# First expert slot prepared during stage one, slot table shared with GpSimd, half slots split like full ones

## The chip, the cores and the metric

The kernel runs on one core of one Trainium2 chip. The metric is the device time of one execution in microseconds; for the kernel before, the median of three runs.

## The reference

Two parts follow each other. The first is a linear-attention recurrence over 768 steps for 4 batches and 8 heads of 40 columns; its output, read as 3072 tokens of 320 columns, is the input x of the second, a mixture of 8 experts with one expert per token:

```
logits = x @ w_gate + modality_bias[modality_id]
e_idx  = argmax(logits, axis=1)
probs  = softmax(logits)          # 1e-09 added to the denominator
gate_w = probs[arange(N), e_idx]
for e in range(8):                # tokens whose expert is e
    h = maximum(x[mask] @ w1[e], 0.0)        # w1[e]: 320 x 1024
    out[mask] = gate_w[mask, None] * (h @ w2[e])   # w2[e]: 1024 x 320
```

All is float32.

## The kernel before, in words

**Stage one** (`phase_a`) computes the recurrence in 24 chunks. Its operations are not issued as they are written: each call is recorded with its operands, and a list scheduler (`Sched.order`) plans all five engines with assumed costs, by the length of the work that follows each operation, and then issues them in that order. Tiles come from rings; a ring made by `late` hands out tiles of stage one that are done with. After every pair of chunks, `gate` (line 990) computes the expert of 256 tokens and scatters their rows, from GpSimd, into a table `xs` in DRAM that is sorted by expert.

**The expert stage** (`_run`, line 1128) works in slots. A full slot is 256 tokens of one expert, a half slot 128. The slots are numbered from -2: slots -2 and -1 are chosen early, at pair 8 of stage one (`early`, line 1076), from the experts that already have 256 tokens; slot 0 after pair 10; slots 1 to 9 (full), 10 and 11 (half) come from a slot table. Slots past 11 stand under a condition at the end (line 1237 on).

A full slot is computed with float32 split in two rounded parts (float32r, high and low), three products for one. `split` (line 1157) makes the parts: for each 128 tokens three transposes of x on TensorE (line 1169) into PSUM, ScalarE copies the high part xh (1171), VectorE subtracts for the low part xl (1172, 1173). For the weights ScalarE copies h (1176, 1180, 1184) and VectorE subtracts for l (1177, 1181, 1185), in pieces named a, b (w1) and c (w2), or q (quarters of w1, for the first slot of a group). Two c pieces of slot -2 are subtracted on GpSimd. The pieces of the next slot are put between the f-steps of the present one by the lists `plan0`, `plan1` and `plan`.

One f-step is 128 of the 1024 hidden columns: `g1` is eight products of 256 columns (line 1201), ScalarE's relu hh (1205), VectorE's low part hl (1206); `g2` is six products of 320 columns (1213 to 1215). `g2` runs two f-steps behind `g1`. `fin` (1216) scales the sum and scatters the rows to the output from GpSimd.

Half slots (`h1`, `h2`, lines 1190 to 1195) are not split: plain float32 products, three of 128 columns and one of 320 for each f-step; TensorE runs a plain float32 product in two instructions.

The slot table (`slots`, line 1031) is 44 small operations on VectorE from the counts of tokens by expert (`cnt`, line 1230). They are issued between the f-steps of slot -2, 15 at a time (`tb`). SP reads the table (`tabi`) for the addresses of slot 1 on.

Slot -2's weights and x are loaded during stage one into the tiles XT0 and BK0 to BK3 (hence their names in the profile), but split only after stage one. Slot -1's weights are loaded when stage one has ended.

Of the kernel before, what the change touches and what calls it, by code (L numbers as in the profile page):

```python
# [71 lines left out]
class Sched:  # L72
# [408 lines left out]
def phase_a(S,ctx,rt,rm,bk,v,w,a,emit_x,pp,ident,kp):  # L481
# [16 lines left out]
    def tiles(name,n,shape,cp=cp): return [cp.tile(shape,F32,name=f"{name}{i}") for i in range(n)]  # L498
# [416 lines left out]
NTL=NT//128; SL=256; NSF=12; NSL=NSF+E; NX0=3; NF0=9; NHF=2  # L915
# [8 lines left out]
class Moe:  # L924
# [106 lines left out]
    def slots(self,ct):  # L1031

        nc=self.nc; V=nc.vector; T=lambda nm,shape,dt=F32: self.wp.tile([128]+shape,dt,name="s_"+nm,bufs=1); NB=NT//SL
# [6 lines left out]
        def run(i):  # L1040
# [3 lines left out]
        le=[lambda k=k,sl=sl,n=n: V.tensor_tensor(c2[:,sl],cur[3][:,k:k+1].broadcast_to([128,n,E]),self.f2[:,0:n].unsqueeze(2).broadcast_to([128,n,E]),op=ALU.is_le) for k,sl,n in part]  # L1044
        return [lambda: V.memset(n0[:,E:],0.0),lambda: V.memset(nh[:,E:],0.0),
            lambda: V.tensor_copy(n0[:,0:E],ct),
            lambda: V.tensor_tensor(n1,ct,self.used[:,0:E],op=ALU.subtract),
            lambda: V.tensor_scalar(m1,n1,-SL/2.0,None,op0=ALU.add),
            lambda: V.tensor_tensor(c1,m1.unsqueeze(2).broadcast_to([128,E,NB]),self.f1.unsqueeze(1).broadcast_to([128,E,NB]),op=ALU.is_gt),
            lambda: V.tensor_reduce(nb[:,0],c1,axis=AX.X,op=ALU.add),  # L1050
            lambda: V.scalar_tensor_tensor(m1,nb[:,0],-float(SL),n1,op0=ALU.mult,op1=ALU.add),
            lambda: V.tensor_scalar(nb[:,1],m1,0.0,None,op0=ALU.is_gt)]+run(0)+run(1)+run(2)+[
            lambda: V.scalar_tensor_tensor(nh[:,0:E],nb[:,0],-float(SL),n0[:,0:E],op0=ALU.mult,op1=ALU.add),
            lambda: V.tensor_tensor(dn[:,0],n0[:,1:E+1],n0[:,0:E],op=ALU.subtract),
            lambda: V.tensor_tensor(dn[:,1],nh[:,1:E+1],nh[:,0:E],op=ALU.subtract),
            lambda: V.scalar_tensor_tensor(dn[:,0],nb[:,0],float(SL),dn[:,0],op0=ALU.mult,op1=ALU.add)]+le+[
            lambda: V.tensor_reduce(es,c2,axis=AX.X,op=ALU.add)]+mul+[
            lambda: V.tensor_scalar(tab[:,NSL:2*NSL],es,float(E-1),None,op0=ALU.min),
            lambda: V.tensor_reduce(s0,c2,axis=AX.X,op=ALU.add),
            lambda: V.tensor_tensor(du,self.used[:,1:E+1],self.used[:,0:E],op=ALU.subtract),  # L1060
            lambda: V.scalar_tensor_tensor(s0[:,0:NSF],self.f2,-float(SL),s0[:,0:NSF],op0=ALU.mult,op1=ALU.add),
            lambda: V.tensor_scalar(tab[:,2*NSL:],cur[3][:,1,E-1:E],float(NF0-NHF),None,op0=ALU.add),
            lambda: V.tensor_tensor(tab[:,2*NSL:],tab[:,2*NSL:],cur[3][:,0,E-1:E],op=ALU.max),
            lambda: V.tensor_scalar(s0[:,0:NSF],s0[:,0:NSF],n0[:,0:1],0.0,op0=ALU.add,op1=ALU.max),
            lambda: V.tensor_scalar(s0[:,NSF:],s0[:,NSF:],nh[:,0:1],None,op0=ALU.add),
            lambda: V.tensor_scalar(s0[:,NSF:NSF+NHF],s0[:,NSF:NSF+NHF],SL/2.0,None,op0=ALU.add)]+le+[
            lambda: V.scalar_tensor_tensor(tab[:,0:NSL],es,float(PT),s0,op0=ALU.mult,op1=ALU.add),
            lambda: V.tensor_tensor(c2,c2,du.unsqueeze(1).broadcast_to([128,NSL,E]),op=ALU.mult),
            lambda: V.tensor_copy(self.tab,tab),
            lambda: V.tensor_reduce(end,c2,axis=AX.X,op=ALU.add),  # L1070
            lambda: V.tensor_tensor(pos,bc(tab[:,0:NSL]),self.row.unsqueeze(1).broadcast_to([128,NSL,2]),op=ALU.add),
            lambda: V.tensor_scalar(end,end,self.used[:,0:1],float(SL),op0=ALU.add,op1=ALU.add),
            lambda: V.scalar_tensor_tensor(end,es,float(PT),end,op0=ALU.mult,op1=ALU.add),
            lambda: V.tensor_tensor(self.pad,bc(end),pos,op=ALU.is_gt),
            lambda: V.tensor_scalar(self.pad,self.pad,float(BIG),None,op0=ALU.mult)]
    def early(self,R):
# [17 lines left out]
        self.first[0]=(idx,xg,r1,r3,r2)  # L1094
# [31 lines left out]
    def _run(self,ctx,wpool,pool,ph,po):  # L1126
# [3 lines left out]
        W_={}; xg=[None]*4; self.wp=wpool  # L1130
        def wt(nm,i,shape,dt=F32): W_[nm,i]=(pool if i==0 else wpool).tile(shape,dt,name=f"{nm}_{i}",bufs=1)
        for i in range(2):
            xg[i]=pool.tile([128,2,XW],F32,name=f"xg{i}",bufs=1)
            wt("r1",i,[128,2,F]); wt("r3",i,[128,F]); wt("r2",i,[128,8,D])
            wt("xf",i,[128,3,128])
            for nm,sh in (("xh",[128,3,SL]),("xl",[128,3,SL]),("h1",[128,2,F]),("l1",[128,2,F]),("w3",[128,F]),("h2",[128,8,D]),("l2",[128,8,D])): wt(nm,i,sh,F32R)
            xg[2+i]=pool.tile([128,2,XW],F32,name=f"xg{2+i}",bufs=1)
        for i in range(2): nc.gpsimd.memset(W_["xl",i][64:128,2].bitcast(F32),0.0)
        def prep(s):
# [3 lines left out]
            hf=half(s); n=SL//2 if hf else SL; k=s-1 if s<=NF0 else s-1-NF0+NSF if hf else s-1-NHF if s<=NSF+NHF else s-1-NF0+NSF-(NSF-NF0)  # L1143
# [5 lines left out]
        half=lambda s: NF0<s<=NF0+NHF  # L1149
# [7 lines left out]
        def split(s,P):  # L1157
            _,x,r1,r3,r2=P
            if half(s):
                xf=W_["xf",s%2]  # L1160
                def xq():
                    tp=ph.tile([128,512],F32,tag="h",name=f"xt{s+2}")[:,0:384].rearrange("p (c t) -> p c t",c=3)
                    for c in range(3): nc.tensor.transpose(tp[0:64 if c==2 else 128,c],x[0][:,(4,132,260)[c]:(132,260,324)[c]],self.ident)
                    nc.scalar.copy(xf[:,0:2],tp[:,0:2]); nc.scalar.copy(xf[0:64,2],tp[0:64,2])
                return (xf,r1,r3,r2),dict(x=[xq],a=[],b=[],c=[],q=[])
# [42 lines left out]
        def g2(s,W,f,hx,os,bs=(0,1)):  # L1208
            if half(s): return h2(s,W,f,hx,os)
            h2_,l2=W[5:]; hh,hl=hx  # L1210
            for b in bs:
# [13 lines left out]
        def group(lo,hi):  # L1225
            P={}; W={}
            if lo<0:
# [5 lines left out]
                for f in u['x']+u['q'][:1]: f()  # L1233
# [159 lines left out]
```

## Time and profile before

| | us |
|---|---|
| runs | 701.68, 703.48, 704.94 |
| median | 703.48 |
| profiled execution | 702.02 |
| its span, first to last instruction | 700.3 |

The page lists for each engine its busy time: PE is TensorE's products, PEld its weight loads, DVE is VectorE, ACT ScalarE, POOL GpSimd, SP the engine that issues DMAs. In names, digits are left out: h and l are the high and low parts of weights, r the raw ones, BK and XT raw ones of slot -2. L391 is the line that issues everything of stage one. Ends of products are modelled; differences of starts are exact.

### The profile page before, as it was taken

To read this page: it belongs to the slowest core of one execution; us is meant where nothing else is said; L and a number is where in the kernel's file an instruction comes from. 1 tells how busy PE (TensorE), PEld (TensorE's weight loads), DVE (VectorE), ACT (ScalarE), POOL (GpSimd) and SP (SyncE) were. 2 spreads that over 40 slices of the span, in tenths; PEclk is the share of its full clock that TensorE was granted. 3 is DMA by queue.
4 is the path that set the end of the run, shared out by engine and by line. 5 is a ranking of instruction groups with operands and counts; after the bars stand their busy time and mean duration, and the time that the engine had idled before them with its cause. 6 is when DMAs were issued, how large, how long until landed. Compare 5 with 4: busy or idle time off the path is not lost.

```text
span 700.3 us, 24925 instructions
## 1 busy us (share of the span) xinstructions
PE 576.2 (82%) x10426; PEld 513.2 (73%) x10426; DVE 461.2 (66%) x1162; ACT 370.2 (53%) x802; POOL 251.5 (36%) x427
## 2 busy tenths in 40 slices
PE   0584679896987699759988987868999999999994
PEld 0473559685766588648876875747999999999972
DVE  5999954266773876395637464359988888888210
ACT  0575233375646746655567375426766666666210
POOL 9467707106958840894180201121111111211110
PEclk9986556787998869867979598757999999999998
DMA  1779422346443636432521336167686777777200
GB/s 46 292 189 239 126 56 70 75 122 184 144 133 79 201 92 148 121 108 61 120 91 44 111 74 218 59 213 204 212 285 206 229 247 230 227 240 223 97 18 12
DMA packets 95721, 102.42 MB, mean 146 GB/s; under 512 B 57775, under 2 KB 78560, under 8 KB 95456
## 3 DMA queue, kind: packets, MB, share of 16 engines
q1 hardware_dynamic: 93200, 92.82, 45.6%
q0 software_dynamic: 2400, 7.92, 3.1%
q8 instruction: 84, 1.38, 0.8%
q14 instruction: 37, 0.30, 0.1%
HBM read 86.38 MB, written 17.52 MB: 148 GB/s over the span
## 4 chain that ended last, share of the span: by engine, by line
PE 51%; DVE 12%; issue 9%; DMA 8%; ACT 4%; POOL 2%; SPq 1%; POOLq 0%; DVEq 0%; ACTq 0%
PE ps_tr L391 24%; PE h L1201 10%; PE ps_rp L391 6%; DMA out_dram<-o,oi 5%; PE os L1215 3%; PE os L1213 3%; PE os L1214 3%; DVE Z L391 2%; PE tz L391 2%; ACT XZ L391 2%; DVE BK L391 1%; PE xt L1169 1%; DMA xs<-xo,pi 1%; SPq L391 1%; DVE qx L391 1%
## 5 line engine op out<-in xcount | busy, mean ns | idle before, releaser
L391 POOL TENSOR_TENSOR tmpP<-L 128x234 f32<-128x234 f32 (+14 forms) x148 | 77.4, 526 | 127.4 <-DMA L<-scr 93.9
L1224 POOL DMA_INDIRECT out_dram<-o,oi x26 | 28.9, 1110 | 172.2 <-DVE oi L1223 97.5
L391 ACT COPY XZ<-BK 32x640 f32<-32x640 f32 x96 | 69.0, 723 | 28.2 <-PE ps_tr L391 25.1
L391 POOL TENSOR_TENSOR L<-L,tmpP 128x234 f32<-128x234 f32 (+14 forms) x148 | 79.7, 542 | 9.0
L1205 ACT ACTIVATE hh<-h 128x256 fp32r<-128x256 f32 x96 | 36.9, 385 | 64.6 <-PE h L1201 64.4
L391 DVE COPY U<-ps_tr 32x320 f32<-32x320 f32 x56 | 27.6, 492 | 52.2 <-PE ps_tr L391 44.2
L1215 PE MATMUL os<-h,hl 128*128 128x320 f32 x192 | 60.1, 313 | 0.7 <-DVE hl L1206 0.7
L1201 PE MATMUL h<-xh,h 128*128 128x256 f32 x192 | 57.3, 298 | 3.8 <-DVE hl L1206 1.5
L1213 PE MATMUL os<-h,hh 128*128 128x320 f32 x192 | 60.3, 314 | 0.0
L1214 PE MATMUL os<-l,hh 128*128 128x320 f32 x192 | 59.9, 312 | 0.0
L391 POOL DMA_INDIRECT xs<-xo,pi x24 | 23.9, 994 | 93.4 <-issue 27.4
L1206 DVE SCALAR_TENSOR_TENSOR hl<-h,hh 128x256 fp32r<-128x256 f32 x96 | 40.6, 423 | 24.2 <-ACT hh L1205 23.2
L1201 PE MATMUL h<-xh,l 128*128 128x256 f32 x192 | 55.4, 289 | 0.3 <-DVE l L1177 0.3
L1201 PE MATMUL h<-xl,h 128*128 128x256 f32 x192 | 55.2, 287 | 0.0
L391 DVE TENSOR_TENSOR MB<-ps_tr,msk 64x512 f32<-64x512 f32 x48 | 33.0, 688 | 30.5 <-PE ps_tr L391 29.8
L391 PE MATMUL ps_tr<-ident,BK 128*104 128x128 f32 x192 | 37.5, 341 | 15.3 <-DVE BK L391 9.3
L391 PE MATMUL ps_tr<-rs,TT 64*64 64x40 f32 x896 | 40.6, 253 | 4.8 <-DMA TT<-scrT 3.3
L391 ACT COPY XZ<-ps_tr 40x320 f32<-40x320 f32 x92 | 38.3, 420 | 11.7 <-PE ps_tr L391 10.4
L391 PEld LDWEIGHTS ps_tr<-rs,TT 64*64 64x64 f32 x896 | 36.5, 162 | 9.4 <-ACT rs L391 2.4
L391 ACT COPY U<-ps_tr 32x320 f32<-32x320 f32 x56 | 23.3, 416 | 37.7 <-DVE U L391 21.2
L391 ACT COPY UT<-ps_tr 104x512 f32<-104x512 f32 x48 | 26.7, 589 | 30.6 <-PE ps_tr L391 30.0
L391 PEld LDWEIGHTS ps_tr<-ident,BK 128*104 128x104 f32 x192 | 27.5, 162 | 19.4 <-DVE BK L391 8.8
(221 smaller groups left out, 1589.1 us busy)
## 6 DMA issues: line engine op xcount, KB each, us to landing
r<-in_moe_w_dram SPq DMA_DIRECT2D x13, 1280.0 KB
r<-in_moe_w_dram SPq DMA_DIRECT2D x13, 1024.0 KB
BK<-in_bk_dram SPq DMA_DIRECT2D x12, 832.0 KB
r<-in_moe_w_dram SPq DMA_DIRECT2D x26, 256.0 KB
A<-in_a_dram SPq DMA_DIRECT2D x12, 416.0 KB
U<-in_v_dram SPq DMA_DIRECT2D x48, 104.0 KB
ws<-in_w_dram SPq DMA_DIRECT2D x24, 165.5 KB
RT<-in_rt_dram SPq DMA_DIRECT2D x48, 80.0 KB
```

Of the source, the lines that this page charges most:

```text
L391: else: r=getattr(getattr(nc,eng),name)(*[rs(x) for x in a],**{n:rs(x) for n,x in k.items()})
L1169: for c in range(3): nc.tensor.transpose(tp[:,c],x[b][:,(4,132,196)[c]:(132,260,324)[c]],self.ident)
L1201: for i,(a,b) in enumerate(k): nc.tensor.matmul(hp,a,b,start=(i==0),stop=(i==len(k)-1))
L1205: nc.scalar.activation(hh,hp,AF.Relu)
L1206: nc.vector.scalar_tensor_tensor(hl,hp,0.0,hh.bitcast(F32),op0=ALU.max,op1=ALU.subtract)
L1213: nc.tensor.matmul(os[b],hh[:,sl],h2_[:,f],start=(f==0),stop=False)
L1214: nc.tensor.matmul(os[b],hh[:,sl],l2[:,f],start=False,stop=False)
L1215: nc.tensor.matmul(os[b],hl[:,sl],h2_[:,f],start=False,stop=(f==7))
L1224: nc.gpsimd.indirect_dma_start(self.out,bass.IndirectOffsetOnAxis(ap=oi.bitcast(U32),axis=0),o,None,bounds_check=NT-1,oob_is_err=False)
```

## The change

1. `early` splits slot -2's x and first-layer weights within stage one, as recorded operations. The parts go into tiles that stage one has done with: AT0 to AT3 (h1, l1 of both halves of w1), XT1 (the last 64 rows), A0 and A1 (xh, xl). These tiles move to the pool `kp`, which lives on, and are taken anew with the type float32r (`Ring.anew`). `_run` starts slot -2 with these tiles; only w2 is still split there.
2. In `slots`, 23 of the 44 operations go to GpSimd (`V`), one to ScalarE; 20 stay on VectorE (`D`). They are issued 7 instead of 15 for each f-step.
3. `h1`, `h2` and the tiles `xf` are gone: half slots are split and computed like full ones, with 128 instead of 256 columns in `g1`, `hh` and `hl`, and one block in `g2`, `fin` and the x part of `split`.
4. The loop in `group` is written more simply; a way of ending a group with a full slot, which does not occur in the group of slots -2 to 11, is left out.

```
 class Ring:
-    alias=None; prior=None
+    alias=None; prior=None; anew=None
+    def get(self,i):
+        if self.anew is not None: self.bufs=[self.anew()]; self.anew=None
+        return self.bufs[i]
...
     def early_tiles():
-        l=[('XT',0)]+[Br[i] for i in OPT['EB']]
-        return [S.late(f"e_{i}",[t]) for i,t in enumerate(l)]
+        l=[('XT',0)]+[Br[i] for i in OPT['EB']]+ATr[:4]+[('XT',1)]+Ar
+        r=[S.late(f"e_{i}",[t]) for i,t in enumerate(l)]
+        for i in range(5,12):
+            tag=f"AT{i-5}" if i<9 else "XT1" if i<10 else f"A{i-10}"; n=2*HQ if i>9 else F
+            r[i].anew=lambda i=i,tag=tag,n=n: kp.tile([128,n],F32R,name=f"er{i}",tag=tag,bufs=1)
+        return r
...
     def slots(self,ct):
-        nc=self.nc; V=nc.vector; ...
+        nc=self.nc; V=nc.gpsimd; D=nc.vector; ...
-            lambda: V.tensor_copy(n0[:,0:E],ct),
-            lambda: V.tensor_tensor(n1,ct,self.used[:,0:E],op=ALU.subtract),
+            lambda: nc.scalar.copy(n0[:,0:E],ct),
+            lambda: V.tensor_tensor(n1,n0[:,0:E],self.used[:,0:E],op=ALU.subtract),
             lambda: V.tensor_scalar(m1,n1,-SL/2.0,None,op0=ALU.add),
-            lambda: V.tensor_tensor(c1,m1.unsqueeze(2)...
-            lambda: V.tensor_reduce(nb[:,0],c1,axis=AX.X,op=ALU.add),
+            lambda: D.tensor_tensor(c1,m1.unsqueeze(2)...
+            lambda: D.tensor_reduce(nb[:,0],c1,axis=AX.X,op=ALU.add),
...
     def early(self,R):
-        self.first[0]=(idx,xg,r1,r3,r2)
+        h1=[S.inst(R[5+2*c],...)...]; l1=[...]; w3=S.inst(R[9],"w3_e",[128,F]); xh,xl=[...]
+        nc.gpsimd.memset(xl[64:128,2].bitcast(F32),0.0); fr=lambda v: v.bitcast(F32R)
+        for b in range(2):
+            tp=S.inst(S.rings['ps_tr'],f"et{b}",[128,3,128]); sl=slice(128*b,128*b+128)
+            for c in range(3): nc.tensor.transpose(tp[:,c],xg[b][:,(4,132,196)[c]:(132,260,324)[c]],self.ident)
+            nc.scalar.copy(fr(xh[:,:,sl]),tp); nc.scalar.copy(fr(xh[0:64,2,sl]),tp[64:128,2])
+            nc.vector.tensor_tensor(fr(xl[:,0:2,sl]),tp[:,0:2],xh[:,0:2,sl].bitcast(F32),op=ALU.subtract)
+            nc.vector.tensor_tensor(fr(xl[0:64,2,sl]),tp[64:128,2],xh[64:128,2,sl].bitcast(F32),op=ALU.subtract)
+        for q in range(2):
+            sl=slice(512*q,512*q+512)
+            for c in range(2):
+                nc.scalar.copy(fr(h1[c][:,sl]),r1[c][:,sl]); nc.vector.tensor_tensor(fr(l1[c][:,sl]),r1[c][:,sl],h1[c][:,sl].bitcast(F32),op=ALU.subtract)
+            nc.scalar.copy(fr(w3[:,sl]),r3[:,sl]); nc.vector.tensor_tensor(fr(w3[64:128,sl]),r3[64:128,sl],w3[64:128,sl].bitcast(F32),op=ALU.subtract)
+        self.first[0]=(idx,xg,r1,r3,r2,(xh,xl,h1,l1,w3))
...
     split:
-            if half(s): ...
-                return (xf,r1,r3,r2),dict(x=[xq],a=[],b=[],c=[],q=[])
+            if s==-2: X=A=B=Q=[]
...
-        def h1(s,W,f): ...
-        def h2(s,W,f,hh,os): ...
-        def g1(s,W,f,to=None):
+        def g1(s,W,f):
-            hp=ph.tile([128,512],F32,tag="h",name=f"h{s+2}_{f}")[:,0:SL]
+            fs=slice(128*f,128*f+128); n=size_(s); ts=slice(0,n)
+            hp=ph.tile([128,512],F32,tag="h",name=f"h{s+2}_{f}")[:,ts]
...
     group:
-                        if lo<0:
-                            for _ in range(MOPT['tb']):
-                                if L: L.pop(0)()
+                    for _ in range(MOPT['tb']):
+                        if L: L.pop(0)()
...
+MOPT.update(tb=7)
```

## Rows read from the trace of the kernel before

**Rows 1.** Page, part 1: busy us (share of the span) and instructions.

```profile
PE 576.2 (82%) x10426; PEld 513.2 (73%) x10426; DVE 461.2 (66%) x1162; ACT 370.2 (53%) x802; POOL 251.5 (36%) x427
```

**Rows 2.** Stretches: us, busy us of PE, PEld, DVE, ACT, POOL; clock, DMA share, GB/s.

```profile
439.50:447.70 8.20, 8.20 (x227) 6.97 (x227) 0.01 (x1) 2.62 (x8) 0.00 (x0) 0.64 0.02 4
466.60:476.90 10.30, 8.58 (x39) 7.88 (x39) 7.16 (x20) 6.35 (x18) 4.55 (x4) 0.54 0.71 226
476.90:494.30 17.40, 13.54 (x77) 12.25 (x76) 16.64 (x61) 9.53 (x23) 1.66 (x1) 0.80 0.64 181
494.30:509.60 15.30, 15.30 (x120) 15.27 (x120) 15.01 (x31) 11.35 (x25) 2.01 (x2) 1.00 0.87 282
509.60:524.90 15.30, 15.30 (x121) 15.28 (x120) 13.27 (x28) 10.09 (x23) 2.35 (x2) 1.00 0.91 283
662.20:675.90 13.70, 13.70 (x77) 10.86 (x76) 1.43 (x5) 2.74 (x10) 1.97 (x2) 1.00 0.04 16
675.90:690.00 14.10, 14.09 (x69) 10.16 (x68) 0.67 (x2) 2.22 (x8) 0.98 (x1) 1.00 0.02 7
```

**Rows 3.** TensorE's timeline: start us, us, instruction [idle before it].

```profile
466.62 0.17 PE L1230 MATMUL cnt<-cum,mones 128*128 128x8 bf16 x1 [0.27 <-DVE pv L391]
469.53 0.58 PE L1201 MATMUL h<-xh,h 128*128 128x256 f32 x1 [1.37 <-ACT h L1176]
470.45 0.58 PE L1201 MATMUL h<-xh,l 128*128 128x256 f32 x1 [0.34 <-DVE l L1177]
...
509.59 0.28 PE L1201 MATMUL h<-xh,h 128*128 128x256 f32 x1
```

**Rows 4.** TensorE's timeline within slot 0: second layer, next first layer.

```profile
510.55 0.31 PE L1213 MATMUL os<-h,hh 128*128 128x320 f32 x1
511.43 0.28 PE L1201 MATMUL h<-xh,h 128*128 128x256 f32 x1
```

**Rows 5.** Timeline of GpSimd and VectorE in slot -2.

```profile
470.49 1.07 POOL L391 DMA_INDIRECT xs<-xo,pi  x1 [0.30 <-issue]
475.31 1.55 POOL L1185 TENSOR_TENSOR l<-BK,h 128x640 fp32r<-128x640 f32 x1 [3.75 <-ACT h L1184]
475.37 1.53 DVE L1048 TENSOR_SCALAR s_m<-s_n 128x8 f32<-128x8 f32 x1
```

**Rows 6.** VectorE's groups in 476.9:494.3: busy us, mean ns, idle before.

```profile
L1181 DVE TENSOR_TENSOR w<-BK,w 64x256 fp32r<-64x256 f32 x2 | 2.1, 1044 | 0.1
L1177 DVE TENSOR_TENSOR l<-BK,h 128x256 fp32r<-128x256 f32 x2 | 0.8, 416 | 0.0
L1042 DVE COPY s_en<-s_en 128x4 f32<-128x4 f32 x1 | 0.2, 170 | 0.0
```

**Rows 7.** GpSimd's groups, whole run: one of its smallest operations.

```profile
L391 POOL TENSOR_TENSOR tmpP<-L 64x14 f32<-64x14 f32 x4 | 1.4, 356 | 0.0
```

**Rows 8.** VectorE's groups in a full slot, 509.6:524.9.

```profile
L1185 DVE TENSOR_TENSOR l<-r,h 128x640 fp32r<-128x640 f32 x5 | 4.2, 835 | 0.0
L1206 DVE SCALAR_TENSOR_TENSOR hl<-h,hh 128x256 fp32r<-128x256 f32 x9 | 3.8, 421 | 1.3 <-ACT hh L1205 1.2
L1177 DVE TENSOR_TENSOR l<-r,h 128x512 fp32r<-128x512 f32 x4 | 2.7, 683 | 0.1
L1181 DVE TENSOR_TENSOR w<-r,w 64x512 fp32r<-64x512 f32 x2 | 1.4, 690 | 0.1
L1172 DVE TENSOR_TENSOR xl<-xt,xh 128x256 fp32r<-128x256 f32 x2 | 0.8, 424 | 0.5 <-ACT xh L1171 0.5
```

**Rows 9.** TensorE's timeline in the half slots: two first layers, twelve f-steps apart.

```profile
668.01 1.02 PE L1192 MATMUL h<-xf,r 128*128 128x128 f32 x6
...
687.16 1.02 PE L1192 MATMUL h<-xf,r 128*128 128x128 f32 x6
```

**Rows 10.** Weight loads in a half slot.

```profile
672.91 0.30 PEld L1192 LDWEIGHTS h<-xf,r 128*128 128x128 f32 x2
```

**Rows 11.** SP's queue near the end of stage one.

```profile
448.01 1.00 SPq L1122 DMA_DIRECT2D BK<-xs  x2
```

More of the change, by code (lines that the diff above doesn't have):

```diff
@@ L1130, in _run @@
         W_={}; xg=[None]*4; self.wp=wpool
+        f=lambda v: v.fn(v.inst.ring.get(v.inst.buf))
+        t=self.first[0][5]; W_["xh",0],W_["xl",0]=f(t[0]),f(t[1]); W_["h1",0],W_["l1",0]=[[f(v) for v in x] for x in t[2:4]]; W_["w3",0]=f(t[4])
         def wt(nm,i,shape,dt=F32): W_[nm,i]=(pool if i==0 else wpool).tile(shape,dt,name=f"{nm}_{i}",bufs=1)
@@ L1157, in split @@
         def split(s,P):
[L1158 to L1164, printed above, removed]
-                return (xf,r1,r3,r2),dict(x=[xq],a=[],b=[],c=[],q=[])
+            _,x,r1,r3,r2=P[:5]
             hT,lT,h1,l1,w3,h2,l2=[W_[n_,s%2] for n_ in ("xh","xl","h1","l1","w3","h2","l2")]
@@ L1207, in g1, with g2, fin @@
             return hh,hl
[L1208 to L1211, printed above, removed]
+        def g2(s,W,f,hx,os):
+            h2,l2=W[5:]; hh,hl=hx
+            for b in blocks(s):
                 sl=slice(128*b,128*b+128)
-                nc.tensor.matmul(os[b],hh[:,sl],h2_[:,f],start=(f==0),stop=False)
+                nc.tensor.matmul(os[b],hh[:,sl],h2[:,f],start=(f==0),stop=False)
                 nc.tensor.matmul(os[b],hh[:,sl],l2[:,f],start=False,stop=False)
-                nc.tensor.matmul(os[b],hl[:,sl],h2_[:,f],start=False,stop=(f==7))
-        def fin(s,P,os,bs=(0,1)):
+                nc.tensor.matmul(os[b],hl[:,sl],h2[:,f],start=False,stop=(f==7))
+        def fin(s,P,os):
             s_,x=P[:2]
-            for b in bs[:len(x)]:
+            for b in blocks(s):
                 o=wpool.tile([128,D],F32,tag="o",name=f"o{s+2}_{b}",bufs=MOPT["ob"])
@@ L1239, in group, with out, do @@
             pend=[]
+            def out():
+                a,ff,h_,o_=pend.pop(0); g2(a,W[a],ff,h_,o_)
+                if ff==7: fin(a,P[a],o_)
+            def do(u,l):
+                for k,i in l:
+                    if i<len(u[k]): u[k][i]()
             for s in range(lo,hi):
                 PL=MOPT['plan' if s>=0 else 'plan1' if s==-1 else 'plan0']
-                os=[po.tile([128,D],F32,tag=f"os{b}",name=f"os{s+2}_{b}") for b in range(1 if half(s) else 2)]
+                os=[po.tile([128,D],F32,tag=f"os{b}",name=f"os{s+2}_{b}") for b in blocks(s)]
                 if s+1<hi: W[s+1],u=split(s+1,P[s+1])
-                last=s==hi-1 and lo<0 and not half(s)
-                to=[W_[n_,(s+1)%2] for n_ in ("h1","l1")] if last else None; bs=(0,) if last else (0,1); hs=[]
                 for f in range(8):
-                    hx=h1(s,W[s],f) if half(s) else g1(s,W[s],f,to); hs.append(hx)
+                    hx=g1(s,W[s],f)
                     if s==lo:
-                        for k,i in MOPT['own'][f]: own[k][i]()
-                        if lo<0:
-                            for _ in range(MOPT['tb']):
-                                if L: L.pop(0)()
+                        do(own,MOPT['own'][f])
+                    for _ in range(MOPT['tb']):
+                        if L: L.pop(0)()
                     pend.append((s,f,hx,os))
-                    if len(pend)>MOPT['lag']:
-                        a,ff,h_,o_=pend.pop(0); b_=bs if a==s else (0,1); g2(a,W[a],ff,h_,o_,b_)
-                        if ff==7: fin(a,P[a],o_,b_)
-                    if s+1<hi:
-                        for k,i in PL[f]:
-                            if i<len(u[k]): u[k][i]()
-                    if f==(MOPT['pf0'] if s<-1 else 6 if s==lo else MOPT['pf']) and s+2<hi: P[s+2]=prep(s+2)
-            for a,ff,h_,o_ in pend:
-                g2(a,W[a],ff,h_,o_,bs)
-                if ff==7: fin(a,P[a],o_,bs)
-            if last:
-                for f in range(8): g2(s,W[s],f,hs[f],os,(1,))
-                fin(s,P[s],os,(1,))
+                    if len(pend)>MOPT['lag']: out()
+                    if s+1<hi: do(u,PL[f])
+                    if f==(MOPT['pf0'] if s<-1 else 6 if s==lo else MOPT['pf']) and s+2<hi: P[s+2]=prep(s+2)
+            while pend: out()
         def first(i):
@@ L1270, in first @@
             if i: return idx,x,*weights(-1,self.val[1,1])
-            r1,r3,r2=self.first[0][2:]
+            r1,r3,r2=self.first[0][2:5]
             return idx,x,[f(v) for v in r1],f(r3),[f(v) for v in r2]
```

82 lines of the change are left out of this document (37 added, 45 removed).

## The prediction

> **What bounds the kernel now.** Read the page first [rows 1]: TensorE is busy 82% of the span and is the longest engine. Then the table of stretches [rows 2], which shows three different limits. From 494.3 on a full slot takes 15.30 us with TensorE busy for all of it at clock 1.00; VectorE has 13 to 15 us of work in it and ScalarE 10 to 11. Before that, the first two slots of the expert stage (slots -2 and -1) are not limited so. In 476.9:494.3 VectorE is busy 16.64 of 17.40 us, TensorE 13.54 at a mean clock of 0.80. In 466.6:476.9 the clock is 0.54. The timeline of TensorE [rows 3] gives the ends of this region: the count product starts at 466.62, slot -2's first product at 469.53, its second at 470.45 (it waits for VectorE), and slot 0's first at 509.59. Two full slots cost 30.6 us; these two take 43.0 from the count. So 12.4 us lie there, in three parts: 3 to 4 us until products flow, the half clock, and VectorE. At the end, 662.2 to 690.0, TensorE is busy throughout with VectorE at 1.43 and 0.67 us of 14: the half slots are bound by TensorE alone.
>
> **The front, counted by TensorE.** The change takes six transposes and the first copies and subtractions out from between 466.62 and 470.45. Products can flow from about 466.8. The two slots then need 30.6 us at full clock. The clock row of 466.6:476.9 (0.54, so some 0.8 of 10.3 us at 1.00) puts the rise near 476.1, 6.6 us after the first product. I assume the same 6.6 us after the change; at half speed they cost 3.3 us. TensorE alone would so reach slot 0 at 466.8 + 30.6 + 3.3 = 500.7, against 509.6: 8.9 us earlier. Slot -1's weights and x are no limit by this trace: its splits wait for VectorE, not for a transfer. Slot 0's load stays queued on SP behind the last scatter, which is unchanged.
>
> **The front, counted by VectorE.** What leaves it: slot -2's split, eight l at 0.416, four w (two at 1.044, two taken like an l) and the xl (1.4, below), together 7.7 us; and 24 of the 44 slot-table operations (23 to GpSimd, one to ScalarE), 23 x 0.17 = 3.9 us, and 1.53 instead of 0.17 for m1 [rows 5, 6]. That is 13 us of records, more than TensorE can use. What limits it is the new waiting. GpSimd ends its last scatter at 470.49 + 1.07 = 471.6 [rows 5]. Only then come four small table operations; the nearest row for one is 0.356 [rows 7], in the sum 0.3. So VectorE's first table operation, c1, starts near 472.7, with hl of f=1 and f=2 queued behind it on VectorE; TensorE wants these at about 475, so nothing is lost. GpSimd then does one l2 quarter, 1.6 us, and eight small operations, 2.4 us: to 476.7. VectorE's dn and le operations wait for that, hl of f=3 stands behind them, and TensorE wants it near 479. From 476.7 VectorE has to do, until slot -2's program is through: 15 table operations (3.2), slot -1's split (four l of 0.683, two w of 0.69, four l2 of 0.835, and xl in two of 0.424 and two short ones, estimated 0.3: 8.9 by [rows 8]), one l2 (0.8) and five hl (2.1): 15.0 us of records. Records overlap a little, each starting before the one ahead has ended; at nine tenths, an estimate, it is 13.5, plus some 2 us of waits for GpSimd's mul, s0 and c2: 492.2. The first hl of slot -1 follows at 492.5. TensorE without stalls would want it at slot -1's start, 485.4, plus three first-layer and two second-layer steps. A first-layer step is 510.55 - 509.59 = 0.96 us and a second-layer one 511.43 - 510.55 = 0.88 [rows 3, 4], which gives 490.0. So TensorE loses about 2 to 2.5 us there; I take 2. After that VectorE has 13.3 us in each 15.3 us slot and catches up. Slot 0 starts at 502.7: **the front gives 6.9 us.** The ends: 8.9 if no wait shows, and 2.0 if all of GpSimd's 23 operations at 0.3 are waited out one by one (509.6 - 500.7 - 6.9).
>
> GpSimd and VectorE also get into each other's way: m1 on VectorE took 1.53 us, beside 0.17 for its like, while GpSimd's l2 ran from 475.31 to 476.86, and the two w took 1.044 on average in this stretch, 0.69 for twice the columns in a quiet slot [rows 5, 6, 8]. The Trainium skill ("SBUF — State Buffer", on the shared port pair) says that the two share a pair of ports as an exclusive lock, which a VectorE operation with two SBUF inputs meets when GpSimd reads SBUF; the rows agree. By that rule the 23 moved operations would still hold VectorE up, which is the second rival.
>
> **The half slots.** Now one f-step, six passes of layer 1 and two of layer 2, takes (687.16 - 668.01)/12 = 1.596 us [rows 9]. After the change it is eight products with 128 moving columns and three with 320. The 320 ones are in the trace: 0.88/6 = 0.147, so 0.44. A 128-column product in this format is not. Its weight load is: two loads of 128x128 behind each other take 0.30 with 0.19 for one, so they start 0.11 apart [rows 10]. From above, the same product with 256 columns takes 0.96/8 = 0.12. Between 0.11 and 0.12, close together, I take 0.114: it is limited by the weight load. Step: 8 x 0.114 + 0.44 = 1.353, so 16 steps gain 16 x 0.242 = 3.9 us; the last step adds a VectorE operation (hl) ahead of its products, 0.4. **The tail gives 3.5 us.** Its cover: in slot 10 VectorE must split slot 11's weights, 8.1 us with one block of x, eight hl (at 128 columns, estimated 0.3: 2.4) and slot 9's output (two of 320 columns, between 0.42 and 0.68, and two short ones: 1.4): 11.9 of records, some 11.3 of time, against 8 x 1.353 + 0.3 = 11.1 on TensorE. It just about fits, and two steps of lag take up the rest. In slot 9 VectorE rises from 5.37 us to the 13.3 of any full slot, in 15.3.
>
> **Stage one.** It gets six transposes, ten ScalarE copies and ten VectorE subtractions, on VectorE 5.5 us by the same rows, on ScalarE about as much. Around them VectorE works 0.01 us and ScalarE 2.62 in 439.5:447.7, where the weights are there; x is loaded at 448.01 [rows 2, 11], and its transposes fall in the stretch that ends with the count. Each can hold a link of that chain by up to 0.6 us, and the whole order of stage one is planned anew. Bounds -0.5 and +3.5 (five or six copies of 0.6 in the way); I take **+0.5**, as the idle time is there and the new work is last in priority. The moved tiles and the loops' rewriting cost nothing: the order of slots is the same.
>
> **Sum.** -6.9 - 3.5 + 0.5 = -9.9 us. The profiled execution took 702.0 (span 700.3 and 1.7 around it), so 692.1; the median of the three runs is 703.5, and on that footing 693.6. I forecast the median: **693.6 us**.
>
> **Rivals.**
> (1) The weight load hides and only the moving columns count. For it: 256 to 320 columns adds 0.027, so 128 would be 0.067. Against it: the 0.11 between loads. Step 0.98; slot 11 takes 7.8, slot 10 is bound by VectorE at 11.3; 19.1 against 25.5 (16 x 1.596), less 0.3: 6.1 instead of 3.5, so 691.0. The Trainium skill ("TensorE: Matmul & The Clock Gate", Back-to-back issue gap) gives 81 ns for a product of 128 columns in a stream with its weight loads; by that figure, as an estimate, it would be 691.9. No run here shows it.
> (2) The table's chain through GpSimd holds VectorE, and hl behind it, so that a wait replaces the work removed. For it: the 1.53 and 1.044 above. Front 2.0 instead of 6.9: 698.5.
> (3) Stage one is longer, by copies in front of its chain or because the first slot's split is not done at 466.6: +3.5 gives 696.6, and from 10 on nothing is left.
> (4) A 128-column product costs no less than the unsplit form does: 0.16 (0.11 of load and then 0.053 of columns) to 0.22 (a quarter of the column rate). Steps of 1.72 to 2.2: 699.5 to 707, at the middle 703.
> (5) **Slower:** TensorE's clock falls to its half level in the half slots, where columns stream only half of the time of layer 1. For it: in 439.5:447.7 TensorE is busy 8.20 of 8.20 us and is granted 0.64. Against it: the half slots now run at 1.00. A step would be twice 1.353, 2.71, and 16 steps 17.8 more than now: 703.5 - 6.9 + 0.5 + 17.8 + 0.4 = 715. It decides once 7 or 8 of the 16 steps are at the low level (9.9/1.353).
>
> **How the numbers follow.** Forecast 0.45, rivals (1) 0.13, (2) 0.15, (3) 0.12, (4) 0.10, (5) 0.05. About 3.5 us (0.5%) either side of 703.5 cannot be told from no change. Below 700: all of the forecast and (1), 0.12 of (2), 0.08 of (3), 0.02 of (4): 0.80. Within: 0.03, 0.03 and 0.05 of (2), (3), (4): 0.11. Above: the rest, 0.09. Range: down to rival (1) with the front at TensorE's bound, 691.0 - 2.0, and a little of stage one, 688; up to 703, which leaves out rival (5) and parts of (3) and (4). Nearly all lies on one side.
>
> **What would show it.** In the trace of after: the count product and then at once slot -2's first layer, no transposes between; slot 0's first product 33 to 37 us after the count (43.0 now); the 128-column products 0.11 to 0.12 apart, at clock 1.00 until the last; slots 10 and 11 together near 24 us from slot 10's first product to the end of the products (27.8 now); the count product no later than 468. Wrong: products of 128 columns at 0.16 or more, GpSimd's table operations as what VectorE waits for through most of slot -2, or the count at 470.

## The result, and the profile after

The changed kernel takes 681.47 us, median of four executions (680.01 to 692.63); the kernel before took 703.41 beside it. The ratio is 0.968, 95% interval 0.964 to 0.972; ratios here and below leave out executions more than 1.5% above the fastest of their kernel. Forecast were 693.6 us and a range of 688 to 703: the sign was right, but the gain is a little over twice what was forecast, and the time lies below the range.

The profiled execution took 680.13 us, its span 678.4, against 702.0 and 700.3. To find the 21.9 us the span is cut at the same five instructions in both traces: SP's first load of U (start-up), the count product, slot 0's first product, slot 10's first, and the end of the last product. In us:

| stretch | before | after | difference | forecast |
|---|---|---|---|---|
| start-up, to the first U load | 30.24 | 22.61 | -7.6 | 0 |
| stage one, from there to the count | 436.38 | 434.15 | -2.2 | +0.5 |
| front, count to slot 0 | 42.98 | 34.82 | -8.2 | -6.9 |
| middle, slots 0 to 9 | 152.62 | 152.55 | -0.1 | 0 |
| tail, slots 10 and 11 | 27.78 | 23.57 | -4.2 | -3.5 |
| last outputs | 10.32 | 10.73 | +0.4 | 0 |

Front and tail gained somewhat more than predicted. A third gain of like size stands in the first 30 us, where the prediction had looked at nothing.

The busy times of after (page, part 1) answer to [rows 1]: TensorE works 15 us less, VectorE 8 us more.

```profile
PE 561.3 (83%) x10474; PEld 505.4 (74%) x10474; DVE 469.3 (69%) x1172; ACT 380.1 (56%) x817; POOL 254.8 (38%) x450
```

The stretches of after, with the columns of [rows 2] (us; busy us of PE, PEld, DVE, ACT, POOL; clock, DMA share, GB/s): slot -2 up to the rise of the clock, the rest of slot -2, slot -1, slot 0, and the two slots of the tail. The front has the clock at 1.00 from 462.0 on. In the tail VectorE has 10.78 and 3.98 us of work and TensorE is busy for all of it.

```profile
456.70:462.00 5.30, 5.24 (x26) 5.24 (x26) 2.43 (x9) 2.06 (x5) 3.09 (x5) 0.53 1.00 362
462.00:474.50 12.50, 11.06 (x83) 10.53 (x82) 10.31 (x29) 10.40 (x22) 7.64 (x20) 1.00 0.73 188
474.50:491.60 17.10, 16.14 (x121) 15.36 (x120) 16.52 (x35) 9.96 (x23) 2.77 (x4) 1.00 1.04 319
491.60:506.80 15.20, 15.20 (x119) 15.19 (x119) 13.15 (x28) 9.99 (x23) 2.19 (x3) 1.00 1.00 288
644.10:656.00 11.90, 11.90 (x100) 11.90 (x98) 10.78 (x24) 8.15 (x21) 2.01 (x2) 1.00 0.05 19
656.00:667.70 11.70, 11.70 (x96) 11.43 (x94) 3.98 (x13) 2.83 (x9) 0.97 (x1) 1.00 0.03 10
```

TensorE's timeline of after answers to [rows 3] and [rows 9]: the count, slot -2's first products 0.02 us behind it with no transposes between, the first of slot 0; then the first four products of an f-step of slot 11 and the first of the next.

```profile
456.76 0.17 PE L1238 MATMUL cnt<-cum,mones 128*128 128x8 bf16 x1 [0.27 <-DVE pv L394]
456.78 5.29 PE L1212 MATMUL h<-er,er 128*128 128x256 f32 x24
...
491.58 0.63 PE L1212 MATMUL h<-er,er 128*128 128x256 f32 x4
...
656.00 0.22 PE L1212 MATMUL h<-xh,h 128*128 128x128 f32 x1
656.06 0.28 PE L1212 MATMUL h<-xh,l 128*128 128x128 f32 x1
656.17 0.28 PE L1212 MATMUL h<-xl,h 128*128 128x128 f32 x1
656.28 0.27 PE L1212 MATMUL h<-xh,h 128*128 128x128 f32 x1
...
657.32 0.22 PE L1212 MATMUL h<-xh,h 128*128 128x128 f32 x1
```

**The start-up, before.** No group of the rows ahead shows it. These are VectorE, GpSimd and SP in a second trace of the unchanged kernel before (start us, us, instruction [idle before it]). The set-up of the gate's bias is one chain: modality_id is loaded, cast (mf, GpSimd), transposed, turned into m and 1 - m (VectorE), and multiplied and added into tbias (GpSimd). The load is there early, but mf stands on GpSimd behind the clears of AT and ATb and starts at 10.10. VectorE waits 6.33 us for it. Its next operation, 1 - m on 24 columns, takes 4.40 us. The last operation of tbias ends at 20.28, behind more clears. BK's first load follows at 20.31: BK's tiles lie in the pool kp, in memory that the set-up's temporary tiles used first (with kp opened ahead of the set-up, in e3, BK is loaded at 5.60).

```profile
10.76 0.18 DVE L966 COPY m<-mtp 128x24 f32<-128x24 f32 x1 [6.33 <-PE mtp L964]
10.98 4.40 DVE L967 TENSOR_SCALAR m<-m 128x24 f32<-128x24 f32 x1
15.48 2.65 DVE L524 MEMSET ps_tr<- 128x512 f32 x5
...
19.13 0.78 DVE L391 TENSOR_TENSOR_SCAN qx<-ws,d1q 128x330 f32<-128x330 f32 x1
```

```profile
7.41 2.73 POOL L391 MEMSET ATb<- 128x1024 f32 x3
10.10 0.28 POOL L960 CAST mf<-mi 24x128 f32<-24x128 int32 x1
10.32 0.94 POOL L391 MEMSET Z<- 128x1024 f32 x1
...
13.51 1.83 POOL L391 MEMSET RT<- 128x1024 f32 x2
15.40 0.98 POOL L391 MEMSET MB<- 32x512 f32 x2
...
18.78 1.50 POOL L971 TENSOR_TENSOR tbias<-tbias,tb 128x192 f32<-128x192 f32 x1
```

```profile
20.31 0.80 SPq L391 DMA_DIRECT2D BK<-in_bk_dram  x2
...
29.99 0.84 SPq L391 DMA_DIRECT2D U<-in_v_dram  x2
```

**The start-up, after** (the same engines). AT0 to AT3, A and XT1 now lie in kp as well. So their clears wait until the set-up is through, and the chain is ahead of them in GpSimd's queue: mf at 5.20, 1 - m in 0.18 us, tbias done at 8.38, and only then the clears of AT. VectorE's first scan is 6.3 us earlier, BK's load 11.5. In all twelve traces the first U load comes 9.7 to 9.9 us behind the later of these two: behind BK in before, e2 and e7, behind the scan in after and the others.

```profile
5.86 0.18 DVE L973 COPY m<-mtp 128x24 f32<-128x24 f32 x1 [4.16 <-PE mtp L971]
6.08 0.18 DVE L974 TENSOR_SCALAR m<-m 128x24 f32<-128x24 f32 x1
...
12.81 0.78 DVE L394 TENSOR_TENSOR_SCAN qx<-ws,d1q 128x330 f32<-128x330 f32 x1
```

```profile
5.20 0.28 POOL L967 CAST mf<-mi 24x128 f32<-24x128 int32 x1 [1.60 <-DMA mi<-in_moe_modality_id_dram]
...
7.79 0.59 POOL L978 TENSOR_TENSOR tbias<-tbias,tb 128x192 f32<-128x192 f32 x1
8.43 1.84 POOL L394 MEMSET AT<- 128x1024 f32 x2
```

```profile
8.78 0.90 SPq L394 DMA_DIRECT2D BK<-in_bk_dram  x2
...
22.61 0.84 SPq L394 DMA_DIRECT2D U<-in_v_dram  x2
```

### The profile page after: what moved, and what is told of

Read it like the earlier page. It is cut to its first block, busy times and chain, and to the rows that moved or that the text cites. A ratio compares the mean times of both kernels' runs of the same rounds, so it can differ in the third digit from the quotient of the medians.

```text
span 678.4 us, 25084 instructions
## 1 busy us (share of the span) xinstructions
PE 561.3 (83%) x10474; PEld 505.4 (74%) x10474; DVE 469.3 (69%) x1172; ACT 380.1 (56%) x817; POOL 254.8 (38%) x450
## 4 chain that ended last, share of the span: by engine, by line
PE 52%; DVE 12%; issue 8%; DMA 6%; POOL 5%; ACT 4%; SPq 1%; POOLq 0%; DVEq 0%; ACTq 0%
PE ps_tr L394 21%; PE h L1212 11%; PE ps_rp L394 5%; PE os L1223 4%; PE os L1221 4%; PE os L1222 4%; PE tz L394 2%; POOL tmpP L394 2%; ACT XZ L394 2%; DMA xs<-xo,pi 2%; DVE Z L394 2%; POOL L L394 2%; DMA L<-scr 2%; DMA out_dram<-o,oi 1%; DVE BK L394 1%
## 5 line engine op out<-in xcount | busy, mean ns | idle before, releaser
L1214 ACT ACTIVATE hh<-h 128x256 fp32r<-128x256 f32 (+1 forms) x112 | 41.3, 369 | 69.5 <-PE h L1212 66.1
L1223 PE MATMUL os<-h,hl 128*128 128x320 f32 x208 | 64.7, 311 | 2.4 <-DVE hl L1215 2.4
L1221 PE MATMUL os<-h,hh 128*128 128x320 f32 x208 | 65.3, 314 | 0.0
L1212 PE MATMUL h<-er,er 128*128 128x256 f32 (+1 forms) x448 | 64.4, 289 | 0.0
L1215 DVE SCALAR_TENSOR_TENSOR hl<-h,hh 128x256 fp32r<-128x256 f32 (+1 forms) x112 | 45.2, 404 | 24.0 <-ACT hh L1214 22.8
L1212 PEld LDWEIGHTS h<-er,er 128*128 128x128 f32 x448 | 59.8, 197 | 0.3 <-issue 0.3
L394 PE MATMUL ps_tr<-ident,BK 128*104 128x128 f32 (+1 forms) x198 | 38.8, 344 | 14.2 <-DVE BK L394 7.6
L1202 DVE TENSOR_TENSOR l<-r,h 128x640 fp32r<-128x640 f32 x52 | 42.7, 824 | 3.3 <-ACT h L1201 2.4
L394 PE MATMUL ps_tr<-ident,Z 128*104 128x128 f32 x184 | 34.0, 312 | 10.6 <-DVE Z L394 7.0
L394 ACT COPY XT<-ps_tr 104x512 f32<-104x512 f32 x48 | 26.9, 585 | 27.4 <-PE ps_tr L394 24.1
```

The lines of the kernel that those rows point to most:

```text
L1202: (nc.gpsimd if s==-2 and q in MOPT['oc'] else nc.vector).tensor_tensor(l2[:,sl],r2[q],h2[:,sl].bitcast(F32),op=ALU.subtract)
L1215: nc.vector.scalar_tensor_tensor(hl,hp,0.0,hh.bitcast(F32),op0=ALU.max,op1=ALU.subtract)
L1221: nc.tensor.matmul(os[b],hh[:,sl],h2[:,f],start=(f==0),stop=False)
L1223: nc.tensor.matmul(os[b],hl[:,sl],h2[:,f],start=False,stop=(f==7))
```

## The experiments

Executions of one kernel spread widely (before: 688.9 to 706.7 us in 19 on one chip), so medians are over all of them, and each conclusion rests first on the stretches of the trace. In us:

| kernel | start-up | stage one (clock) | front | middle | tail | profiled | median (n) | before beside it (n) | ratio, interval |
|---|---|---|---|---|---|---|---|---|---|
| before | 30.24 | 436.38 (0.78) | 42.98 | 152.62 | 27.78 | 702.02 | | | |
| b2_before | 29.99 | 439.65 (0.79) | 42.78 | 152.62 | 27.78 | 704.94 | 704.94 (1) | 702.40 (7) | |
| after | 22.61 | 434.15 (0.80) | 34.82 | 152.55 | 23.57 | 680.13 | 681.47 (4) | 703.41 (4) | 0.968, 0.964 to 0.972 |
| a2_after | 22.41 | 440.66 (0.77) | 34.81 | 152.55 | 23.56 | 686.41 | 681.94 (4) | 702.40 (7) | 0.968, 0.958 to 0.978 |
| e1_tiles | 22.49 | 432.06 (0.80) | 42.82 | 152.54 | 27.78 | 689.96 | 688.93 (10) | 697.86 (19) | 0.993, 0.989 to 0.998 |
| e2_setup_v | 21.84 | 429.82 (0.82) | 42.81 | 152.62 | 27.78 | 686.78 | 687.65 (10) | 697.86 (19) | 0.992, 0.988 to 0.997 |
| e3_kpfirst | 21.66 | 430.93 (0.79) | 34.86 | 152.67 | 23.59 | 676.08 | 676.01 (4) | 697.86 (19) | 0.976, 0.969 to 0.983 |
| e6_nosplit | 22.38 | 427.75 (0.82) | 41.37 | 152.55 | 23.57 | 679.27 | 681.43 (4) | 697.86 (19) | 0.986, 0.976 to 0.997 |
| e4_halves | 22.60 | 433.15 (0.81) | 34.71 | 152.54 | 27.78 | 682.76 | 683.18 (4) | 702.40 (7) | 0.976, 0.968 to 0.984 |
| e5_table_v | 22.55 | 441.33 (0.78) | 34.60 | 152.55 | 23.56 | 686.74 | 683.16 (6) | 702.40 (7) | 0.966, 0.957 to 0.976 |
| e7_m_tt | 29.48 | 433.15 (0.81) | 44.28 | 152.63 | 27.78 | 699.37 | 700.03 (10) | 704.85 (13) | 0.993, 0.988 to 0.999 |
| e8_best | 20.19 | 441.36 (0.76) | 34.82 | 152.66 | 23.59 | 685.15 | 683.48 (4) | 704.85 (13) | 0.967, 0.961 to 0.972 |

**e1_tiles: the tiles alone.**

```diff
+ (A, AT0 to AT3 and XT1 in kp, as in the change)
+er=[self.kp.tile([128,n],F32R,name=f"er{i}",tag=g,bufs=1) for i,(g,n) in enumerate([("AT0",F), ...])]
+W_["h1",0],W_["l1",0],W_["w3",0]=er[0:4:2],er[1:4:2],er[4]; ...
```

> The kernel before with one edit: the tiles AT0 to AT3, A0, A1 and XT1 lie in the pool kp, and slot parity 0 of the expert stage takes its h1, l1, w3, xh and xl from them; nothing is split early, table and half slots are those of before. Stage one's order on every engine is that of before but for GpSimd's and VectorE's first 30 instructions. Theory A (start-up: the clears of AT in kp wait for the set-up's temporary tiles, so the set-up chain goes ahead of them on GpSimd): first U load near 22.6 us instead of 30.2, count product near 457.5 instead of 466.6, the front (count to slot 0) 43.0 and the tail 27.8 as before; 694 us. Theory B (stage one is shorter because it is planned anew with the early split's operations in it): count at 466.6, 703.5 us.

Start-up 22.49: theory A, and B falls. Behind the first clears stage one's order is that of before, and front and tail are those of before. The count came at 454.55, earlier than the 457.5 expected, by stage one's scatter. The median is 8.9 us below that of before; the ratio, which leaves the longest executions out, shows less: 0.993. GpSimd's cast and first clear of AT:

```profile
5.08 0.28 POOL L960 CAST mf<-mi 24x128 f32<-24x128 int32 x1 [1.48 <-DMA mi<-in_moe_modality_id_dram]
...
8.55 1.84 POOL L391 MEMSET AT<- 128x1024 f32 x2
```

**e2_setup_v: the cause without the tiles.**

```diff
-mf=...; nc.gpsimd.tensor_copy(mf,mi[:,:,0])
+mf=...; nc.vector.tensor_copy(mf,mi[:,:,0])
-nc.gpsimd.tensor_tensor(self.bias, ...)   # and t2, and their sum
+nc.vector.tensor_tensor(self.bias, ...)
```

> The kernel before with the set-up's cast of modality_id (mf) and the three operations of tbias on VectorE instead of GpSimd; all tiles where they were. Theory A: what costs the start-up is that these four stand behind clears in GpSimd's queue. mf goes from 10.1 to about 5.3 us, the first BK load from 20.3 to about 9, the first scan on VectorE from 19.1 to 10.5 to 13, the first U load from 30.2 to 21 to 24, count 457 to 460; 694 to 697 us. Theory A2 (the clears on GpSimd hold VectorE up wherever the chain stands, as in the 4.40 us of m's second operation): that operation stays above 3 us and half of the gain is lost, 699. Theory B: no change, 703.5.

Much the same gain, start-up 21.84, with every tile where it was. So what counts is where the chain stands in GpSimd's queue, and the place of the tiles only by that: mf at 4.96, the first scan at 10.90, BK at 12.07 (about 9 had been expected). The operation on m took 0.20; it fell just ahead of a run of clears, so A2 was not put to the test here. The count came at 451.66, earlier than expected; the median is 10.2 us below before.

```profile
4.96 0.23 DVE L960 CAST mf<-mi 24x128 f32<-24x128 int32 x1 [0.53 <-DMA mi<-in_moe_modality_id_dram]
...
5.87 0.20 DVE L967 TENSOR_SCALAR m<-m 128x24 f32<-128x24 f32 x1
...
10.90 0.78 DVE L391 TENSOR_TENSOR_SCAN qx<-ws,d1q 128x330 f32<-128x330 f32 x1
```

**e7_m_tt: the 4.40 us alone.**

```diff
-nc.vector.tensor_scalar(m1[:,0],m1[:,1],-1.0,1.0,op0=ALU.mult,op1=ALU.add)
+nc.vector.tensor_tensor(m1[:,0],on,m1[:,1],op=ALU.subtract)   # on: a tile of ones
```

> The kernel before with one instruction of the set-up in another form: m = 1 - m as a TENSOR_TENSOR on VectorE (a tile of ones minus m) instead of a TENSOR_SCALAR, which took 4.40 us in before while GpSimd ran its clears behind each other. Theory A (the form is what is locked out): by the Trainium skill, SBUF - State Buffer, on the shared port pair, two SBUF inputs meet GpSimd's lock only where GpSimd reads SBUF, and a clear reads nothing; 0.2 to 0.4 us, and the first scan comes at 14.9 instead of 19.1. Theory B (any VectorE operation that begins beside these clears is locked out): 4 us or more again. For the start-up: if VectorE's chain sets it, the first U load moves from 30.2 to 26 and the time by 4.2 us; if the BK loads set it, which wait for tbias on GpSimd (20.3), the U load stays at 29 to 30 and the time stays.

The operation takes 0.18 beside the same clears, as theory A has it, and VectorE's first scan is at 14.91. But the first U load is at 29.48: BK's load, which waits for tbias, is still at 19.81. Two chains hold the start-up, and freeing one is worth 0.5 to 0.8 us. The front was 1.3 us longer: 25 us behind the count the clock falls for 3.4 us (0.51 in 487.6:491.0, with TensorE busy throughout), where before runs at 1.00 (491.6:495.0); by these rows that costs up to 1.7 us, an estimate. The median is 4.8 us below before, more than the start-up gives; where the rest comes from is not explained, and it is no more than stage one scatters.

```profile
10.98 0.18 DVE L967 TENSOR_TENSOR m<-on,m 128x24 f32<-128x24 f32 x1
...
14.91 0.78 DVE L391 TENSOR_TENSOR_SCAN qx<-ws,d1q 128x330 f32<-128x330 f32 x1
```

```profile
19.81 0.80 SPq L391 DMA_DIRECT2D BK<-in_bk_dram  x2
...
29.48 0.84 SPq L391 DMA_DIRECT2D U<-in_v_dram  x2
```

**e3_kpfirst and e8_best: going on from after.** In e3 the pool kp is opened ahead of the set-up's temporary pool; in e8 mf is also cast on VectorE.

```diff
+kp=ctx.enter_context(tc.tile_pool(name="kp",bufs=1))
 with ExitStack() as c1:
     ptr=...; M=Moe(...)
-kp=ctx.enter_context(tc.tile_pool(name="kp",bufs=1))
```

> The kernel after with the pool kp opened ahead of the set-up's temporary pool, so that kp's tiles no longer wait for the set-up. Two AT clears on GpSimd and two on VectorE go back ahead of the set-up chain, the four ATb clears stay behind it. Theory A (what counts is where the chain mf to tbias stands, and what VectorE and GpSimd do behind it): the chain itself starts within 1 us of where it stands after (5.2), the AT clears now fill idle time of both engines, and GpSimd's and VectorE's later start-up comes 2 to 2.8 us earlier; count 454 to 455, 679 us. If instead the waiting of kp for the set-up is itself what made it fast (clears ahead of the chain are what costs): mf near 8 us and half of the 9.9 us lost, 686.

> The kernel after with kp opened ahead of the set-up's temporary pool and the set-up's cast mf on VectorE. The cast goes from 6.4 (with kp first alone) to 5.0 us, the first scan from 11.85 to 10.4 to 10.8, the first U load from 21.7 to 20.2 to 20.7 (22.6 in after); front 34.8, middle 152.6, tail 23.6 as after; stage one anywhere between 428 and 441; 673 to 682 us. Risk: m's second operation falls beside the clears on GpSimd and takes up to 4 us; then the U load is at 24 and it is slower than after.

In e3 mf starts at 6.41, not at 5.2 as expected; behind it the engines have less left to do, and the start-up is 0.95 us shorter than after, not 2 to 2.8. In e8 it is 2.4 shorter, as expected; but stage one came at 441.36 and the median, 683.48, lies above the 673 to 682 expected. Neither is shown to be faster than after as a whole: the ratios to before by plain medians are 0.969 (e3), 0.970 (e8), 0.969 and 0.971 (after, twice). All beat before.

**e6_nosplit and e5_table_v: the two parts of the front.** In e6 slot -2 is split behind the count as before; in e5 the whole slot table runs on VectorE.

```diff
-nc=self.nc; V=nc.gpsimd; D=nc.vector; ...        # e5
+nc=self.nc; V=D=nc.vector; ...
-            if s==-2: X=A=B=Q=[]                 # e6, with the split taken out of stage one
```

> The kernel after without the early split: slot -2's x, h1, l1 and w3 are split behind the count product as before, into the same reused tiles; slot table and half slots as after. Theory A: stage one as after, count at 456.8 give or take 1; the front is longer by the six transposes and the split on VectorE, 40 us instead of 34.8 (43.0 before); 686.5 us. Theory B (the early split's operations are what shortens stage one): count back at 466, 696 us. If the early split gave the front nothing and the table did it all: front 35, 681.5.

> The kernel after with all operations of the slot table on VectorE and none on GpSimd or ScalarE; early split and half slots as after. Without the early split the table on GpSimd was worth 1.6 us (front 41.4 instead of 43.0). Theory of the prediction (VectorE has too much to do until slot -1): 23 operations of 0.17 come back, 3.9 us of records, and TensorE loses 1.5 to 3 us more: front 36.3 to 37.8. Rival (the chain through GpSimd costs the waits that it saves in records): front 34.8 or less, no change.

Without the early split the front is 41.37, without the table's move 34.60, with both 34.82. So beside the table's move the early split gives 6.5 us, and beside the early split the table's move gives nothing; alone the move gives 1.4 to 1.6 (before, twice: 42.98 and 42.78). In e5 the rival came true. In e6 the count came at 450.12, not 456.8 or 466: its theory B falls. The first rows are e6's: transposes follow the count at once, the first product waits 1.37 us for a copy, the next for VectorE, and slot 0 starts at 491.49. The last two are the ends of e5's front.

```profile
450.12 0.17 PE L1221 MATMUL cnt<-cum,mones 128*128 128x8 bf16 x1 [0.27 <-DVE pv L394]
450.15 1.52 PE L1170 MATMUL xt<-ident,BK 128*128 128x128 f32 x6
453.04 0.58 PE L1195 MATMUL h<-er,er 128*128 128x256 f32 x1 [1.37 <-ACT er L1177]
453.95 2.29 PE L1195 MATMUL h<-er,er 128*128 128x256 f32 x9 [0.34 <-DVE er L1178]
...
491.49 0.75 PE L1195 MATMUL h<-er,er 128*128 128x256 f32 x5
```

```profile
463.88 0.17 PE L1238 MATMUL cnt<-cum,mones 128*128 128x8 bf16 x1 [0.27 <-DVE pv L394]
...
498.48 0.75 PE L1212 MATMUL h<-er,er 128*128 128x256 f32 x5
```

**e4_halves: the half slots as before.**

```diff
-hx=g1(s,W[s],f)
+hx=(u1 if half(s) else g1)(s,W[s],f)   # u1: full precision on unsplit tiles, as before
```

> The kernel after with the two half slots computed as before: two passes in full precision on unsplit weights and x, no VectorE in them. By the trace of after (tail 23.57 instead of 27.78) 4.2 us slower than after, f-step 1.596 again; by the prediction's term 3.5. Start-up, front and middle as after.

Tail 27.78 instead of 23.57: 4.2 us, in every digit that of before. The median, 683.18, is only 1.2 us above that of after beside it (681.94): medians of four executions do not settle differences of this size, and the stretch does.

**b2_before and a2_after: the same two kernels again.**

> The kernel before once more, unchanged, for a second trace. The traces so far split the span into start-up (to the first U load), stage one, front, middle and tail. If the time between the first U load and the count product is what varies between executions (the executions of this kernel spread from 689 to 707 us in the last comparison), start-up 30.2, front 43.0, middle 152.6 and tail 27.8 come again to 0.3 us, and only stage one differs from 436.4, by up to 10 us, with as much difference in the time at the half clock. If the start-up is what varies, the first U load is off 30.2 by more than 1 us.

> The kernel after once more, unchanged, beside the others of this comparison. Start-up 22.6, front 34.8, middle 152.6, tail 23.6 again to 0.3 us; stage one between 427 and 437; 675 to 682 us, 15 to 20 us below the kernel before on the same chip. If the 9.9 us by which the count product came earlier were all the change's, its count is again at 456.8 give or take 1.

Start-up, front, middle and tail come again to 0.25 us; stage one came at 439.65 and 440.66, where it had been 436.38 and 434.15. After's count, 463.07, was not again at 456.8, and stage one lies above the 427 to 437 expected. That the time at the half clock goes with it, as expected of b2, did not hold for this pair: its stage one was 3.3 us longer at a mean clock of 0.79 instead of 0.78. So the 2.2 us by which after's stage one was shorter in the first pair of traces are no effect of the change that can be told from the scatter. As an estimate, with the difference between the profiled execution and the median put down to stage one, it is 437.8 (before) and 435.5 (after) in the first comparison, 437.1 and 436.2 in the second. On the chip of e1, e2, e6 and e3 it is 431.0, 430.7 and 429.9 without the early split and 430.9 with it. No cost of the early split in stage one shows; one of about 1 us could not be seen.

## Why the prediction was wrong

**The step that failed** is the one on stage one, and in it the sentence "The moved tiles and the loops' rewriting cost nothing: the order of slots is the same." The order of slots is, and so, apart from the added operations and a few neighbours, is that of stage one behind its start. But moving tiles between pools moved their clears in GpSimd's queue behind the set-up chain, and that is worth 7.6 us (e1; e2 by the other way). The estimate of +0.5, with bounds -0.5 and +3.5, was drawn from stage one's last 27 us alone, where the new operations go; it had no term for the first 30 us of the span. This one term took the time out of the range: without it, 703.4 less the other 14.3 us is 689.1, inside it. A tile that takes over memory brings a wait, which the prediction never asked for. Reading the first 30 us would have shown VectorE waiting 6.3 us and then busy 4.40 us on 24 columns.

**The front**, -8.2 instead of -6.9, was right on the early split and mis-sized. Products follow the count by 0.02 us, not 0.2. Then the prediction adds 3.3 us for the half clock and 2 for stalls. In the trace of after the clock rises 4.9 us after the first product and stays, which costs 2.5, and 34.8 - 30.5 - 2.5 = 1.8 us of stalls are left: together 4.3 instead of 5.3. But the two are not terms that can be added. In e3 the clock rises 6.1 us behind the count, in e4 3.4, which is worth 1.4 us of TensorE's time, and the fronts are 34.86 and 34.71: TensorE waits 2.2 us for VectorE's hl in e3 and 2.9 in e4. Most of what an earlier rise gives goes into waiting for VectorE, so it is no gain of the change.

What was wrong is the part that VectorE's relief by the table was given in it: e5 puts these operations back, VectorE has 31.4 us of work in the front instead of 29.3, and the front is no longer. In after VectorE waits for GpSimd's table operations four times, 2.65 us in all, and in e5 not once, so that what the move saves in records it loses in waits: rival (2) in small. The stretches are the fronts of after and e5, with the columns of [rows 2]; the rows are VectorE's waits in after.

```profile
456.70:491.60 34.90, 32.44 (x226) 31.13 (x226) 29.27 (x72) 22.43 (x49) 13.50 (x27) 0.93 0.92 279
463.90:498.50 34.60, 32.03 (x226) 30.19 (x226) 31.35 (x95) 22.36 (x48) 7.07 (x6) 0.96 0.93 284
```

```profile
461.30 0.26 DVE L1056 TENSOR_TENSOR s_c<-s_m,f 128x96 f32<-128x96 f32 x1 [0.44 <-POOL s_m L1055]
464.90 0.17 DVE L1063 SCALAR_TENSOR_TENSOR s_dn<-s_en,s_dn 128x8 f32<-128x8 f32 x1 [0.99 <-POOL s_dn L1061]
468.22 0.32 DVE L1066 TENSOR_REDUCE s_s<-s_c 128x20 f32<-128x160 f32 x1 [0.57 <-POOL s_c L1050]
474.78 0.18 DVE L1080 SCALAR_TENSOR_TENSOR s_end<-s_es,s_end 128x20 f32<-128x20 f32 x1 [0.65 <-POOL s_end L1079]
```

**The half slots**, -4.2 instead of -3.5. The 128-column products are 0.111 us apart (0.114 had been taken); the first of a step is followed after 0.06. An f-step is (665.32 - 656.00)/7 = 1.331, and 16 x (1.596 - 1.331) = 4.2. The last step's extra VectorE operation, put at 0.4, does not show, and the tight cover of slot 10 by VectorE held: TensorE is busy for all of 644.1:656.0. Rivals (1) and (4) did not come. The Trainium skill's 81 ns ("TensorE: Matmul & The Clock Gate", Back-to-back issue gap) is too low for this stream of float32r products, where 111 were measured. The clock stayed at 1.00 to the last product, so rival (5) is out too.

**The sum.** Start-up -7.6, front -8.2, tail -4.2: 20.0 of the 21.9 us. The rest lies in stage one's scatter and the last outputs; rival (3), a longer stage one, does not show.

## What to carry to other kernels

When a tile is moved to another pool, ask what used that memory first and what the tile's first writer now waits for; the answer may reorder a queue far from the edit. Read the first microseconds of a span as closely as its bound stage: a chain of small operations behind clears cost 7.6 us here, and no share of busy time shows it. Work that is taken off one engine is a gain only if its answers do not come back over a longer road: the table on GpSimd was worth nothing beside the early split. Where two chains end at the same point, find out which is later before one is shortened: in e7, 4.2 us taken from the earlier one gave 0.5 to 0.8.

## What the runs showed of the hardware

- VectorE's TENSOR_SCALAR on 24 columns stood for 4.40 us, from 10.98 to 15.38, while GpSimd cleared tiles behind each other until 15.34 (two traces); its end falls into the first gap between two clears, 15.34 to 15.40. As a TENSOR_TENSOR in the same place it took 0.18 (e7). The Trainium skill ("SBUF — State Buffer", SBUF: two separate sides) has the shared port pair as an exclusive lock and counts an operation with two SBUF inputs only against a GpSimd operation that reads; the TENSOR_TENSOR of e7 agrees. The TENSOR_SCALAR has one input, as has m1 in [rows 5], which took 1.53 us beside GpSimd's subtraction: the prediction's sentence on two inputs covers neither, and the rows show that they wait.
- Stage one, with nearly the same order on every engine, took 427.7 to 441.4 us in twelve traces, and on the whole it goes with TensorE's granted clock, which changes there between its levels (1.2 and 2.4 GHz): 0.82 on average in the shortest, 0.76 in the longest. GpSimd's work in it is the same, 198 and 197 us. Which of the two, time or clock, follows the other is not shown.
- At the full level slots 0 to 9 repeat to 0.13 us in 152.6, in every kernel.
